# First query product of a fused attention and feed-forward kernel: plain loads ahead of transposing loads, chunk 0 transposed on TensorE, first product kept in SBUF

## The chip, the core and the metric

The kernel runs on one core of a Trainium2 chip. The core has TensorE (PE in the profile, with its weight loads as PEld), VectorE (DVE), ScalarE (ACT), GpSimd (POOL) and SyncE (SP), each with an instruction queue of its own that is worked off in order. Transfers are issued from the queues of SP, ACT and POOL. The metric is device time in microseconds (us) of one execution. Before the change three executions took 722.78, 722.94 and 723.15 us; the median is 722.94 us.

## The reference

All tensors are bf16; S = 2048 rows, D = 1024, 32 heads of 32, Df = 3584.

```python
qkv = (x @ wqkv)                       # 2048x1024 @ 1024x3072, cut into q, k, v
# each position attends to itself and 7 positions 2, 4, .. 14 rows back
logits = einsum("bhsd,bhswd->bhsw", q, kg) * scale
a = einsum("bhsw,bhswd->bhsd", softmax(logits), vg) @ wo
b = (gelu(x @ w_gate) * (x @ w_up)) @ w_down
g = sigmoid((x * gate_w).sum(-1, keepdims=True))
out = g * a + (1 - g) * b
```

## The kernel before

**Tiling.** The rows are cut into four chunks of 512. A contraction tile is 128 wide, so D has eight of them (kt 0 to 7). Matmuls take the transposed activations: `xs[c]` holds chunk c of x as eight 128x512 tiles.

**Fast products.** Every large product is done by a seven-product block scheme instead of eight: two blocks of rows (chunk 0 and chunk 1 for the first pair), two halves of the contraction, two halves of the columns. It needs sums and differences of blocks. For the activations these are T1 (`tf[:, 0]`, chunk 1 first half minus chunk 0 first half, L516), T2 (L518), T3 (L520) and T4 (L521), all on DVE (`x_forms`). For the weights they are four forms, each written by DVE in two instructions for the qkv weights (`qkv_forms`, L709). Partial results are carried from one product to another by copies: a PSUM bank is seeded with an earlier product, or a copy in SBUF is added on the way out.

**The first query product.** `first_pair` (L568) runs the scheme for q of chunks 0 and 1, over four column tiles t. In order: A, first half of the contraction (kt 0 to 3, L592); a copy of A into a second bank Bk, the seed (L602 on DVE, L604 on ACT); A, second half (kt 4 to 7); the gate's products of chunks 0 and 1 (`gate`, L874, with a transposing read of the bank by DVE, L880); then the products with T1 (Dk, copied to SBUF by L637), T2 (Bk, copied by L648), T3, the fourth weight form, and T4 (all matmuls at L772). After that follow k and v for the same chunks, the feed-forward pass of the first two chunks from about 84 us on, and the second pair.

**What feeds it.** Two plain loads (`load_rows`, L312, on SP's and ACT's queues) bring the first half of chunk 0's columns as rows; `turn_rows` (L543) transposes them on TensorE with an identity (L550), 16 transposes into four banks, one row tile each, and copies them out (L559, L561). `loads` (L424) then issues on SP's queue, in this order: the query weights kt 0-1 and kt 2-3 (512 KB each, L428), a transposing load of the second half of chunk 0 (L357), kt 4-5 and kt 6-7, two transposing loads of chunk 1 (L357), eight key weight tiles (L352), the value weights (L434) and the first rows of w_down (L387).

**The order of the work.** The instruction order on every engine is made when the kernel is built. `Weave.run` (L134) keeps eleven streams of operations, with an estimated cost and the dependencies of each, and emits the operation that could start earliest, with a bias per stream or operation and due times for the weight forms (`DUE`, L224). Each engine keeps that order. A change at the start therefore shifts the planner's clocks and can alter the order on DVE, ACT, SP and POOL in the rest of the kernel. In the second pair (from about 309 us) the stages repeat for chunks 3 and 2, with the sums L837 and L847 read out of the banks by DVE, and attention work (L937, L943, L1084, L1094) between them on the same queue.

Of the kernel before, what the change touches and what calls it, by code (L numbers as in the profile page):

```python
# [14 lines left out]
P = 128  # L15
# [139 lines left out]
def kernel(  # L155
# [152 lines left out]
    def xb_give(i, op):  # L308
        xb_free.append((i, op))

    def load_rows(q, j, hf):
        q.dma_start(out=hrow[:, XR + j:XR + j + 2, hf * KH * P:(hf + 1) * KH * P],  # L312
                    in_=x[j * P:(j + 2) * P, hf * KH * P:(hf + 1) * KH * P].rearrange("(j p) n -> p j n", p=P))

    load_rows(nc.sync, 0, 0)
    load_rows(nc.scalar, 2, 0)
    grow = xbuf[0:KT, 1, 0:P]
    nc.scalar.dma_start(out=grow, in_=gate_w.rearrange("(k p) -> k p", p=P))
    warm = xbuf[:, 0, 0:2]
# [32 lines left out]
            yield ring_load(("wqkv", c, which, kt), lambda g, kt=kt: nc.sync.dma_start(  # L352
                out=g.rearrange("p (k n) -> p k n", k=1), in_=qkv_src(which, kt, 1)), deps)

    def early_x(c):
        for hf in range(2) if c else (1,):
            o = Op("SP", (KH * P * SC * 2, 2.1), lambda hf=hf: nc.sync.dma_start_transpose(  # L357
                out=xq(c, hf), in_=x[c * SC:(c + 1) * SC, hf * KH * P:(hf + 1) * KH * P]), tail=1.2)
            yield o
            for k in range(KH):  # L360
                w.done[("x", 1, KH * hf + k) if c else ("pt", k, 1)] = o

    def load_x(c, deps):
        deps = deps + ([[("qk", 1)], [("att", 0)]][c - 2] if c > 1 else [])
# [8 lines left out]
    def load_prep(i0):  # L373
        n = min(2, NPREP - i0)
        kind, src, nr = ("d", B_w_down, FH) if i0 < FH else ("o", A_wo, NTH)
        r0 = i0 if kind == "d" else i0 - FH
        si = i0 // 2 % NSTG

        def fn():
            st = stage(si)  # L380
            for h, r in ((0, r0), (1, nr + r0)):
                if kind == "d":
                    v = src[r * P:(r + n) * P, :].rearrange("(k p) (h n) -> p k h n", p=P, h=2)
                else:
                    v = AP(src.tensor, src.offset + r * D, [[NT * D, P], [D, n], [NW, 2], [1, NW]])
                for k in range(n):
                    nc.sync.dma_start(out=st[:, 2 * h + k], in_=v[:, k])  # L387
        return Op("SP", (4 * n * P * NW * 2, 2.0 * n), fn, [("preps", i0 - 2 * NSTG)] if i0 >= 2 * NSTG else [("qkv", 1, 0, t) for t in range(NT)] if si == 2 else [("gcol",)] if si == 1 else [],
                  key=("prep", i0))

    def load_block(sup, b, first=()):
# [30 lines left out]
                    ([("stored", "o" if o else "d")] if name[0] == "T" else []) + [("w", 0, NBLK - 1, 3)] + list(first))  # L422

    def loads():  # L424
        for kt in range(0, KT, 2):
            if kt == KH:
                yield from early_x(0)
            o = Op("SP", (2 * P * D * 2, 0.7), lambda kt=kt: nc.sync.dma_start(  # L428
                out=qbuf[:, kt:kt + 2], in_=qkv_src(0, kt, 2)), key=("wqkv", 0, 0, kt))
            yield o  # L430
            w.done["wqkv", 0, 0, kt + 1] = o
        yield from early_x(1)
        yield from load_qkv(0, 1)
        yield Op("SP", (KT * P * D * 2, 1.0), lambda: [nc.sync.dma_start(out=vbuf[:, hf * KH:(hf + 1) * KH],  # L434
                                                                        in_=qkv_src(2, hf * KH, KH)) for hf in range(2)],
                 key=("wqkv", 0, 2))
        yield load_prep(0)
        yield load_prep(2)
        yield from load_block(0, 0)
        yield load_prep(4)  # L440
        yield from load_block(0, 1)
        for b in range(2, NBLK):
            yield from load_block(0, b)
            if 4 + 2 * (b - 1) < NPREP:
                yield load_prep(4 + 2 * (b - 1))
        for sup in range(NSUP):
            c0 = 2 * sup
            more = sup + 1 < NSUP
            if more:
                yield from load_down(c0)  # L450
                for n in range(3):
                    yield from load_qkv(c0 + 2, QVK[n], range(KT) if n == 0 else [k for i in range(KH) for k in (i, i + KH)],
                                        [("wq", c0 + 2, QVK[n - 1], 3, KH - 1)] if n else [])
                for b in range(NE // FB):
                    yield from load_block(sup + 1, b, [("wq", c0 + 2, QVK[2], 3, KH - 1)])
                yield from load_down(c0 + 1)
                for b in range(NE // FB, NBLK):
                    yield from load_block(sup + 1, b)
            else:
                yield from load_down(c0)  # L460
                yield from load_down(c0 + 1)
# [47 lines left out]
    def x_forms():  # L509
        t = tt(KH * SC)  # L510
        for sup in range(NSUP):
# [1 line left out]
            dx = [("x", max(ca, cb), kt) for kt in range(KT)]  # L513
            b12, b22, b11, b21 = xq(cb, 0), xq(cb, 1), xq(ca, 0), xq(ca, 1)
            free = [("ffn", sup - 1)] if sup else []
            t1 = dve(t, lambda b12=b12, b11=b11: V(out=tf[:, 0], in0=b12, in1=b11, op=ALU.subtract), dx[0:KH] + free, lag=0.5, key=("xf", sup, 1), bias=-1.0)  # L516
            yield t1
            t2 = dve(t, lambda b22=b22: V(out=tf[:, 1], in0=b22, in1=tf[:, 0], op=ALU.subtract), [t1] + dx[KH:], lag=0.5, key=("xf", sup, 2), bias=-1.0)  # L518
            yield t2
            yield dve(t, lambda b12=b12, b22=b22: V(out=b12, in0=b22, in1=b12, op=ALU.subtract), [("z", cb)], key=("xf", sup, 3), bias=-1.0 if sup else -0.3)  # L520
# [19 lines left out]
        yield halo_of(c, kT, 1)  # L540
        yield halo_of(c, vT, 2)

    def turn_rows():  # L543
        for j in range(NST):
            i, free = bank_take()
            pt = banks[i][:].bitcast(BF16)[:, 0:KH * P].rearrange("p (k s) -> p k s", k=KH)

            def go(pt=pt, j=j):
                for kk in range(KH):
                    nc.tensor.transpose(out=pt[:, kk, :], in_=xrow(j, kk, 1), identity=ident)  # L550
            o = Op("PE", 0.24, go, [free] if free else [], tail=0.17)
            yield o
            if j == NST - 1:
                gt = banks[i][:].bitcast(BF16)[:, KH * P:KH * P + KT]
                og = Op("PE", 0.1, lambda: nc.tensor.transpose(out=gt, in_=grow, identity=ident[0:KT, 0:KT]), [], tail=0.17)
                yield og
            dst = xs[0][:, 0:KH, j * P:(j + 1) * P]
            if j % 2:
                e = act(0.58, lambda pt=pt, dst=dst: nc.scalar.copy(out=dst, in_=pt), [o], key=("pt", j, 0))  # L559
            else:  # L560
                e = dve(0.42, lambda pt=pt, dst=dst: nc.vector.tensor_copy(out=dst, in_=pt), [o], key=("pt", j, 0))  # L561
            yield e
            if j == NST - 1:
                e = act(0.2, lambda: nc.scalar.copy(out=gcol[:], in_=gt), [og], key=("gcol",))
                yield e
            bank_give(i, e, True)

    def first_pair(c, prod, dst, ev, B11, B21, T1, T2, T3, B22, T4):  # L568
# [15 lines left out]
            return ap if t < 2 else two(ap)  # L584

        def mm(t, kts):
            d = [("wqkv", c, 0, kt) for kt in kts] + [("x", ca, kt) for kt in kts if ca]                 + [("pt", j, kts[0] // KH) for j in range(NST) if not ca]

            def go():
                for kt in kts:  # L590
# [7 lines left out]
        def seed(t):  # L598
# [6 lines left out]
            yield e  # L605
            ev["seed", t] = fr[t] = e

        if not c:
            for t in ts:
                A[t], fr[t] = bank_take(dirty=True)  # L610
            for kt in range(2):
                for t in ts:
                    yield mm(t, [kt])
        for t in ts:
            if c:
                A[t], fr[t] = bank_take()
            yield mm(t, range(KH) if c else [2, 3])
            yield from seed(t)
        if not c:
            for t in ts:  # L620
                yield mm(t, [KH, KH + 1])
        for t in ts:
            yield mm(t, range(KH, KT) if c else [KT - 2, KT - 1])
            out_, key, d = dst(1, 0, t)
            e = act(0.48, lambda t=t, out_=out_: nc.scalar.copy(out=out_, in_=banks[A[t]][:]), [at[t]] + d, key=key)
            yield e
            bank_give(A[t], e)
        for t in ts:
            if not c and t < 2:
                yield from gate(t)  # L630
            Dk[t], free = bank_take(dirty=t > 1)
            o = prod(Dk[t], 0, 0, T1, t, True, [free])
            yield o

            def cp(t=t):
                m5[t] = hold(t, 0, "m5")
                nc.scalar.copy(out=m5[t], in_=as_(t, banks[Dk[t]][:]))  # L637
            ev["m5", t] = act(0.48, cp, [o])
            yield ev["m5", t]
        for k in range(2):  # L640
            ring_give(("wqf", c, 0, 0, k), o)
        for t in ts:
            o = prod(Bk[t], 0, 1, T2, t, False, [ev["seed", t]])
            yield o

            def cp2(t=t):
                u2[t] = hold(t, 1, "u2")
                nc.scalar.copy(out=u2[t], in_=as_(t, banks[Bk[t]][:]))  # L648
            ev["u2", t] = act(0.48, cp2, [o])
            yield ev["u2", t]  # L650
        for k in range(2):
            ring_give(("wqf", c, 0, 1, k), o)
        for t in ts:
# [96 lines left out]
    def qkv_pair(c, whichs=QVK):  # L750
# [8 lines left out]
                return tmp(which, t), ("tmp", which, t), d  # L759
            return qkv_dst(ca if first else cb, which, t), ("qkv", ca if first else cb, which, t), d  # L760

        def prod(bk, which, form, rhs, t, start, deps):
            def fn():
                for kt in range(KH):
                    if isinstance(form, tuple):
                        hi, up = form
                        wv = qkv_w(c, which, kt + KH * hi)
# [8 lines left out]
            elif isinstance(form, tuple):  # L776
                d = raw_keys(c, which, range(KH * form[0], KH * form[0] + KH))
            else:
                d = [("wq", c, which, form, kt) for kt in range(KH)]
            sup = c // 2  # L780
            have = [[("x", ca, kt) for kt in range(KH * hf, KH * hf + KH)] if ca else [("pt", j, hf) for j in range(NST)] for hf in range(2)]
            d += {(0, 0): have[0], (1, 0): have[1],
                  0: [("xf", sup, 1)], 1: [("xf", sup, 2)], (0, 1): [("xf", sup, 3)], 3: [], (1, 1): [("xf", sup)]}[form]
            return pe(KH, fn, d + [x_ for x_ in deps if x_ is not None])

        if whichs == [0]:
            yield from first_pair(c, prod, dst, ev, B11, B21, T1, T2, T3, B22, T4)
# [609 lines left out]
            w.done[("down", c)] = o  # L1397

    def main():
        yield from turn_rows()  # L1400
        yield from qkv_pair(0, [0])
        yield from qkv_pair(0, [1])
        yield from gate_sum(0)
# [53 lines left out]
```

## Time and profile before

| what | value |
| --- | --- |
| median of three executions | 722.94 us |
| span of the profiled execution, first to last instruction | 720.1 us |
| PE busy | 710.1 us, 99% of the span |
| DVE busy | 609.8 us, 85% |
| ACT busy | 323.8 us, 45% |
| TensorE clock granted | full in all 40 slices |
| PE busy in the first 20.76 us | 15.85 us |
| DMA rate in 20.76 to 35.44 us | 374 GB/s |

The profiled execution's own time is its 720.1 us span and what lies around it; against the median 2.8 us lie outside. The page cuts the span into 40 slices of 18 us and gives each engine's busy tenths; the chain of work that ended last is followed back from the last instruction to what released each step. A busy PE in the first slice includes eight warm-up matmuls (3.43 us) on a zeroed tile.

### The profile page before, as it was taken

The page shows a single profiled execution, that of the slowest core. Times are in us where ns is not written, and L with a number is a line of the kernel's source. Part 1 is how long each engine was busy: PE and PEld are TensorE (multiplying, and loading weights), DVE is VectorE, ACT ScalarE, POOL GpSimd, SP SyncE. Part 2 cuts the span into 40 slices and gives each one's busy share as a digit, 9 for nine tenths or more (in the row PEclk, how much of TensorE's full clock was granted, in tenths as well). Part 3 has the DMA queues.
Part 4 walks back from the last instruction along what each step waited for, and adds up shares of the span by engine and source line. Part 5 has one row for each costly group of instructions (what it writes and reads, how often), then busy time and mean ns, then how long its engine had stood idle before and what let it go on. Part 6 is the DMA issues. An engine that isn't in the chain of part 4 may idle for free.

```text
span 720.1 us, 9892 instructions
## 1 busy us (share of the span) xinstructions
PE 710.1 (99%) x3337; PEld 342.7 (48%) x3337; DVE 609.8 (85%) x862; ACT 323.8 (45%) x547; POOL 73.8 (10%) x130
## 2 busy tenths in 40 slices
PE   7999999999999999999999999999999999999997
PEld 3556544444444444456554444444444444444443
DVE  4989999999998999799789988799999997849300
ACT  3354585555585522153465323258556655310110
POOL 0020333343121100100000000100000000001000
PEclk9999999999999999999999999999999999999999
DMA  9953899996797799943378899996647656999992
GB/s 263 363 192 97 248 295 311 362 317 225 179 249 230 238 253 330 336 174 117 88 214 272 277 299 352 311 310 186 185 137 194 172 165 161 322 294 376 297 338 93
DMA packets 184179, 176.84 MB, mean 246 GB/s; under 512 B 58304, under 2 KB 140224, under 8 KB 184000
## 3 DMA queue, kind: packets, MB, share of 16 engines
q1 hardware_dynamic: 174512, 145.53, 68.6%
q0 software_dynamic: 9328, 30.42, 11.6%
q8 instruction: 26, 0.43, 0.2%
q10 hardware_dynamic: 288, 0.26, 0.1%
q14 instruction: 25, 0.20, 0.1%
HBM read 132.12 MB, written 31.46 MB: 227 GB/s over the span
## 4 chain that ended last, share of the span: by engine, by line
PE 96%; DVE 1%; SPq 1%; DMA 1%; issue 0%; ACT 0%; DVEq 0%
PE ps L1136 47%; PE ps L1305 30%; PE ps L772 18%; PE ps L592 1%; SPq L357 1%; DMA hT<-in_A_wqkv_dram 1%; DVE ring L709 0%; SPq L428 0%; DVE lend L837 0%; DVE tf L518 0%; DVE zt L880 0%; PE ps L874 0%; ACT ost L1346 0%; DVE hT L709 0%; PE ps L898 0%
## 5 line engine op out<-in xcount | busy, mean ns | idle before, releaser
L1136 PEld LDWEIGHTS <-ring 128*128 128x128 bf16 x1568 | 153.2, 98 | 185.1 <-issue 0.5
L1136 PE MATMUL ps<-lend,ring 128*128 128x512 bf16 x896 | 212.7, 379 | 0.0
L1136 PE MATMUL ps<-tf,ring 128*128 128x512 bf16 x672 | 164.3, 379 | 0.0
L1305 PE MATMUL ps<-ring,hT 128*128 128x512 bf16 x708 | 160.7, 379 | 0.0
L1305 PEld LDWEIGHTS <-hT 128*128 128x128 bf16 x708 | 69.1, 98 | 83.8 <-DVE ost L1380 0.4
L1084 DVE TENSOR_TENSOR xbuf<-xbuf,lend 128x2048 bf16<-128x2048 bf16 x64 | 77.5, 1217 | 16.6 <-DMA xbuf<-xbuf 16.5
L772 PEld LDWEIGHTS <-ring 128*128 128x128 bf16 x512 | 65.0, 127 | 49.6 <-issue 3.6
L937 DVE TENSOR_TENSOR xbuf<-qo,lend 128x2048 bf16<-128x2048 bf16 x64 | 77.0, 1218 | 2.3 <-ACT lend L830 2.3
L943 DVE TENSOR_TENSOR xbuf<-xbuf 128x2048 bf16<-128x2048 bf16 x56 | 68.2, 1218 | 0.2
L772 PE MATMUL ps<-tf,ring 128*128 128x512 bf16 x256 | 58.4, 380 | 3.2 <-DVE lend L837 1.4
L772 PE MATMUL ps<-lend,ring 128*128 128x512 bf16 x256 | 57.9, 379 | 0.0
L1346 ACT ACTIVATE ost<-ps,omg 128x512 bf16<-128x512 f32 x16 | 11.0, 687 | 101.3 <-PE ps L1305 89.7
L1168 ACT COPY ps<-ps 128x512 f32<-128x512 f32 x56 | 32.1, 573 | 51.8 <-PE ps L1136 51.6
L1212 ACT ACTIVATE gl<-ps 128x512 bf16<-128x512 f32 x56 | 33.5, 598 | 46.5 <-PE ps L1136 46.3
L1305 PE MATMUL ps<-ring,qo 128*128 128x512 bf16 x192 | 49.3, 380 | 0.0
L1338 POOL DMA_DIRECT2D out_dram<-ost x24 | 13.0, 541 | 336.6 <-ACT ost L1346 248.3
L1185 DVE TENSOR_TENSOR hT<-hT,gl 128x1024 bf16<-128x1024 bf16 x56 | 38.3, 685 | 8.6 <-ACT hT L1178 8.5
L505 POOL DMA_DIRECT2D fforms<-ring x56 | 30.8, 551 | 144.2 <-DVE ring L496 138.1
L1224 DVE TENSOR_TENSOR u<-ps,u 128x512 f32<-128x512 f32 x56 | 38.3, 685 | 2.7 <-PE ps L1136 2.3
L1228 ACT ACTIVATE gl<-u 128x512 bf16<-128x512 f32 x56 | 35.4, 633 | 11.3 <-DVE u L1224 10.7
L1220 ACT COPY u<-ps 128x512 f32<-128x512 f32 x56 | 32.8, 586 | 14.3 <-PE ps L1136 14.3
L1094 DVE TENSOR_TENSOR xbuf<-xbuf 128x2048 bf16<-128x2048 bf16 x32 | 38.9, 1217 | 0.1
(120 smaller groups left out, 668.8 us busy)
## 6 DMA issues: line engine op xcount, KB each, us to landing
ring<-dforms SPq DMA_DIRECT2D x112, 256.0 KB, 5.0
ring<-in_B_w_down_dram SPq DMA_DIRECT2D x84, 256.0 KB, 5.4
ring<-in_B_w_gate_dram SPq DMA_DIRECT2D x56, 256.0 KB, 5.4
fforms<-ring POOLq DMA_DIRECT2D x56, 256.0 KB, 5.2
ring<-fforms SPq DMA_DIRECT2D x56, 256.0 KB, 4.1
ring<-in_B_w_up_dram SPq DMA_DIRECT2D x42, 256.0 KB, 4.8
ring<-in_A_wqkv_dram SPq DMA_DIRECT2D x32, 256.0 KB, 4.5
ring<-oforms SPq DMA_DIRECT2D x32, 256.0 KB, 5.6
```

What stands on the lines that cost most here:

```text
L772: nc.tensor.matmul(banks[bk][:], lhsT=lhsT, rhs=rhs[:, kt, :], start=(start and kt == 0), stop=(kt == KH - 1), skip_group_check=True)
L937: V(out=w3(box[t]), in0=q_b, in1=k_w, op=ALU.mult)
L943: V(out=w3(box[0]), in0=w3(box[0]), in1=w3(box[t]), op=ALU.add)
L1084: return dve(tt(n), taking(("p", t), lambda: V(out=w3(box["p", t]), in0=w3(box["ab"]), in1=v_w, op=ALU.mult)), [("qkv", c, 2, t), abo] + ( ...
L1094: V(out=p0.rearrange("p (u n) -> p u n", u=2), in0=lo, in1=hi, op=ALU.add)
L1136: nc.tensor.matmul(banks[bk][:], lhsT=wv[:, k, fl * P:(fl + 1) * P], rhs=rhs[:, k, :], start=(start and k == 0), stop=(k == KH - 1), skip_ ...
L1185: yield dve(tt(2 * SC), lambda hv=hv, gv=gv: nc.vector.tensor_tensor(out=hv, in0=hv, in1=gv, op=ALU.mult), [e, ev[f, "g1"], ev[f, "g2"]], ...
L1212: nc.scalar.activation(out=gl[f][:, r1 * SC:(r1 + 1) * SC], in_=banks[A[f]][:], func=ACT.Gelu_apprx_tanh)
L1220: nc.scalar.copy(out=u2[f][:], in_=banks[Bk[f]][:])
L1224: e = dve(tt(SC, True), lambda f=f: nc.vector.tensor_tensor(out=u2[f][:], in0=banks[Dk[f]][:], in1=u2[f][:], op=ALU.add), [o, ev[f, "u2"]])
L1228: ev[f, "g2"] = act(0.54, lambda f=f: nc.scalar.activation(out=gl[f][:, r2 * SC:(r2 + 1) * SC], in_=u2[f][:], func=ACT.Gelu_apprx_tanh), [ ...
L1305: nc.tensor.matmul(banks[bk][:], lhsT=l, rhs=wv[:, i, :], start=(start and k == 0), stop=(q == last and i == 1), skip_group_check=True)
```

## The change

- `loads` issues the query weights as eight loads of 256 KB, tile by tile. Between kt 3 and kt 4 a plain load brings the second half of chunk 0 as rows (512 KB, four row tiles), in place of the transposing load. The two transposing loads of chunk 1 stay behind all of these.
- `turn_rows(hf)` now turns one half at a time, and goes by contraction tile: four transposes fill one bank with tile kt of all 512 rows. The first half is copied out by DVE and ACT in turn, the second half, turned within `first_pair`, by DVE alone.
- A, first half, is copied to SBUF by ACT (`keep`, into the last rows of `hT`), not to a second bank. Four further ACT copies bring it from there into the banks Bk once the A banks are free. The two DVE seeds go.
- T1 of the first pair is made in two halves, and the T1 products of t = 0, 1 start on the first half. The gate's product of chunk 1 comes after them, and the T2 product of t = 0 comes ahead of the T1 product of t = 3.
- The first w_down rows wait for the seeds, the second ones for the last turned tile (the buffers are shared).

```diff
-    def early_x(c):
-        for hf in range(2) if c else (1,):
+    def early_x():
+        for hf in range(2):
...
     def loads():
-        for kt in range(0, KT, 2):
+        for kt in range(KT):
             if kt == KH:
-                yield from early_x(0)
-            o = Op("SP", (2 * P * D * 2, 0.7), lambda kt=kt: nc.sync.dma_start(
-                out=qbuf[:, kt:kt + 2], in_=qkv_src(0, kt, 2)), key=("wqkv", 0, 0, kt))
-            yield o
-            w.done["wqkv", 0, 0, kt + 1] = o
-        yield from early_x(1)
+                yield Op("SP", (KH * P * SC * 2, 0.6), lambda: load_rows(nc.sync, 0, NST, 1), key=("xr", 1))
+            yield Op("SP", (P * D * 2, 0.5), lambda kt=kt: nc.sync.dma_start(
+                out=qbuf[:, kt:kt + 1], in_=qkv_src(0, kt, 1)), key=("wqkv", 0, 0, kt))
+        yield from early_x()
...
-            t1 = dve(t, lambda b12=b12, b11=b11: V(out=tf[:, 0], in0=b12, in1=b11, op=ALU.subtract), dx[0:KH] + free, lag=0.5, key=("xf", sup, 1), bias=-1.0)
-            yield t1
+            for k0, n_, key in ((0, KH, ("xf", sup, 1)),) if sup else ((0, KH // 2, ("xfa", sup)), (KH // 2, KH // 2, ("xf", sup, 1))):
+                t1 = dve(tt(n_ * SC), lambda b12=b12, b11=b11, k0=k0, n_=n_: V(
+                    out=tf[:, 0, k0:k0 + n_], in0=b12[:, k0:k0 + n_], in1=b11[:, k0:k0 + n_], op=ALU.subtract),
...
-    def turn_rows():
-        for j in range(NST):
+    def turn_rows(hf):
+        for kk in range(KH):
             i, free = bank_take()
...
+            def go(pt=pt, kk=kk):
+                for j in range(NST):
+                    nc.tensor.transpose(out=pt[:, j * P:(j + 1) * P], in_=xrow(j, KH * hf + kk, 1), identity=ident)
+            o = Op("PE", 0.24, go, ([free] if free else []) + ([("xr", 1)] if hf else []), tail=0.17)
...
             yield mm(t, range(KH) if c else [2, 3])
-            yield from seed(t)
+            if c:
+                yield from seed(t)
+            else:
+                def keep(t=t):
+                    late[t] = hrow[:, FT - 4 + t, :].bitcast(F32)
+                    nc.scalar.copy(out=late[t], in_=banks[A[t]][:])
+                fr[t] = ev["kept", t] = act(0.48, keep, [at[t]])
+                yield fr[t]
         if not c:
-            for t in ts:
-                yield mm(t, [KH, KH + 1])
+            yield from turn_rows(1)
+            for kt in (KH, KH + 1):
+                for t in ts:
+                    yield mm(t, [kt])
...
+            for t in ts:
+                Bk[t], free = bank_take(True)
+                ev["seed", t] = act(0.5, lambda t=t: nc.scalar.copy(out=banks[Bk[t]][:], in_=late[t]), [ev["kept", t]] + ([free] if free else []))
+                yield ev["seed", t]
+            w.done["seeded",] = ev["seed", KH - 1]
+            for kts in ((0, 1), (2, 3)):
+                for t in ts[:2]:
+                    yield from first5(t, kts)
+            yield from gate(1)
+            yield from first5(2)
+            yield from second6(0)
+            yield from first5(3)
+            for t in ts[1:]:
+                yield from second6(t)
```

## The prediction

> **What bounds the kernel now.** I read the slices first. PE is busy in every slice but the first and the last, at full clock.
>
> ```profile
> PE   7999999999999999999999999999999999999997
> DVE  4989999999998999799789988799999997849300
> PEclk9999999999999999999999999999999999999999
> ```
>
> So time can be won where PE waits. PE's own waits after 20 us are two small ones in the second pair, behind DVE's sums, and the one that ends at 20.76 us:
>
> ```profile
> PE ps L772 <- DVE lend L837: 1.4, 2, 0.9
> PE ps L772 <- DVE zt L880: 0.8, 1, 0.8
> ```
>
> The chain of waits of the first 60 us (start, length, what) shows what sets 20.76 us: SP's queue and transfers to 12.73, then DVE without a gap, then PE alone.
>
> ```profile
> 2.27 4.97 SPq L357
> ...
> 7.28 0.58 SPq L428
> ...
> 7.90 4.83 DMA hT<-in_A_wqkv_dram
> ...
> 12.83 1.90 DVE ring L709 x3
> 14.72 0.60 DVE hT L709
> ...
> 17.01 1.18 DVE tf L518
> ...
> 18.72 1.28 DVE ring L709 x2
> ...
> 20.09 0.64 DVE zt L880
> ...
> 20.76 39.01 PE ps L772 x180
> ```
>
> The timeline of PE shows its work ahead of that, with the idle time and what ended it in brackets:
>
> ```profile
> 6.16 3.61 PE L592 MATMUL ps<-lend,hT 128*128 128x512 bf16 x16 [0.67 <-ACT lend L559]
> 11.28 3.67 PE L592 MATMUL ps<-lend,hT 128*128 128x512 bf16 x16 [1.50 <-DMA hT<-in_A_wqkv_dram]
> 16.52 1.05 PE L772 MATMUL ps<-tf,ring 128*128 128x512 bf16 x4 [1.02 <-DVE tf L516]
> 18.05 1.92 PE L772 MATMUL ps<-tf,ring 128*128 128x512 bf16 x8
> ```
>
> From 20.76 PE does the last 68 of the q matmuls and ends the q pair at 35.44: 0.216 us each. What ends q earlier ends the kernel earlier, as long as the later order adds no wait.
>
> **The transfers.** Adding each issue's start to its time to landing: query weights kt 0-1 land at 1.25 + 4.7 = 5.95, kt 2-3 at 1.76 + 5.6 = 7.36, the transposing load of chunk 0 at 2.27 + 7.0 = 9.27, kt 4-5 at 7.28 + 4.0 = 11.28, kt 6-7 at 12.73, chunk 1's halves at 8.41 + 6.4 = 14.8 and 12.6 + 4.2 = 16.8. So 512 KB plain behind another cost 1.41 and 1.45, and 512 KB transposed 1.91, 2.07 and 2.0. kt 4-5 took 2.01 behind the transposing load, 0.58 too long: SP had been held 4.97 us in that load's issue and issued them only at 7.28.
>
> The change puts a plain 512 KB in place of the transposed one (2.0 - 1.43 = 0.57 saved), and nothing on SP holds the weights back (0.58 saved). kt 7 then lands at 12.73 - 1.15 = 11.6, chunk 1 at 13.6 and 15.6. The plain rows land at 7.36 + 1.43 = 8.8. SP issues nine loads where two weight loads and a transposing one stood; at 0.49 us each (eight key loads in 3.90) it is through at 5.8, ahead of the data, so the count costs nothing; if the queue were no longer ahead, each would cost its 0.49. The key weights behind the transposing loads start when the second issue ends, about 1.1 us earlier than 14.81.
>
> [...]
>
> **PE and DVE up to q's end.** All times below are in the profile's clock.
> First half: the rows of ACT's queue land at 0.74 + 3.8 = 4.54, 16 transposes take 1.07 (L550), so A starts at about 5.7; eight matmuls to 7.4, kt 3 landed at 7.36, eight more to 9.2 (3.61 for 16).
> Added: 16 transposes, 1.07, to 10.3. They lie in the time in which PE stood 1.50 for kt 4-5 before; without that cover they would cost their 1.07.
> DVE copies the four turned tiles one after the other (0.42 each, L561) from 9.65 on, to 11.3; the first query weight form follows (0.61), the second starts at 11.9. It stood at 12.83. The data (11.6) is no longer its limit, the copies are. Gain 0.93. If copies follow each other faster than their 0.42, as L709 does (0.61 apart at 0.69 long), it is 1.1; if the rows, which come in shorter pieces, cost 2.0 like a transposed load, kt 7 lands at 12.2 and the gain is 0.5.
> From there DVE's order is as before, in which 7.93 us lie from that form to PE's restart at 20.76. Splitting T1 (1.22 for one) costs a second start, about 0.07. Chunk 1's first half (13.6) is there when DVE comes to T1 at 14.4, its second half (15.6) when it comes to T2 at 16.1. The second gate read then frees its bank at 11.9 + 7.93 + 0.07 = 19.9.
> PE meanwhile: A's second half 10.3 to 14.0 (3.67), gate 0.61; T1's first half is ready at 15.05; T1 products of t = 0, 1 by 16.85 (four times two matmuls, 1.73), second gate to 17.5, t = 2 to 18.3, then the T2 product of t = 0 (0.86) to 19.2, which before came after the wait. T2 is made by 17.3. PE waits 0.7 for the bank and restarts at 19.9 with 64 matmuls left, not 68: 64 x 0.216 = 13.8, end at 33.7. Against 35.44 the gain is 0.86 + 0.86 = 1.7 us.
>
> ACT gains work: four keeps and four seeds of 0.57 in place of two copies, with the four q copies between them. The last q copy ends at about 14.7, the first seed at 15.3, the last at 17.0; they are wanted at 18.3 and after 20.8, and the first Dk copy queued behind them is ready only at 17. Cover 3.0 us on the first seed; beyond it each us costs one. DVE loses two copies of 0.70. The w_down rows that now wait for the seeds (17.0) were issued at 20.73, behind the value weights; 1.1 us off that is still later than 17.0, so nothing.
>
> **Later.** PE's order is the same after the first pair. On DVE, ACT, SP and POOL the order is replanned. k's forms had their last key weights at about 23.9 (issued 18.2, 5.7 to landing) and k starts at 35.44; DVE idles 2.29 us at 40.0 to 42.3, so k and v keep up with a PE that comes 1.7 earlier. In the second pair the operations in the changed order between the first q form (before at 308.65) and the first L837 add up to 35.2 us by the rows of before, against 35.1: the wait of 0.94 there stays. It could go, with the 0.44 at 369 (-1.4); or DVE could come later by one attention transposing issue (two took 5.03), +2.5. I take 0, because the sums agree. POOL's stores have nobody waiting at once.
>
> Sum: 720.1 - 1.7 = 718.4 span; the 2.8 us around it stay, so 722.9 - 1.7 = 721.2.
>
> **Rivals.**
> 1. The start gains little. For: chunk 1's transposing loads now stand behind 3.1 MB of plain data, and T1 has 0.8 us of slack on them. If they land at their old 14.8 and 16.8, T1 starts 0.4 later than I have it, T2 0.7 later; with the rows at 2.0 us as well, 0.5 to 0.9 of the gain is left: 722.2. Against: the landings are evenly spaced behind one another in one queue.
> 2. More than I count: both waits behind L837 go too. 721.2 - 1.4 = 719.8. For: the query weights of the second pair are now loaded ahead of two attention transposing loads, before behind them. Against: T2 of the second pair comes behind later pieces of chunk 3 now, so DVE starts no earlier.
> 3. Slower: a new wait in the second pair. The last two value weight tiles stand on SP behind two transposing loads that wait for the probabilities on DVE. I place these at 316, the two issues take 5.03, landing about 5 later, 326; DVE's form wants them at about 328.6. Slack 2.5; every further us moves L837, and PE already waits there, so it costs one. It decides above 2.5 + 1.7 = 4.2 us late; 6 late gives 721.2 + 3.5 = 724.7. Against: no such slip of SP in the profile of before, whose loads end their waits at DVE forms, not at PE.
>
> **How the numbers follow.** The main case has 0.55, its own range 720.4 to 722.0 (start gain from 0.9 to 2.5). Rival 1 has 0.21, rival 2 0.13, rival 3 0.11. A measurement tells about 0.2%, 1.45 us, from no change, so faster means under 721.5: 0.41 of the main case and rival 2, together 0.54; slower than 724.4 is most of rival 3, 0.10; the rest, 0.36, is within. The range reaches over rival 2 to 719.5 and over rival 1 to 723.1, the slowest of the three executions before (a start that gains nothing); it leaves out rival 3 and the far ends of the others.
>
> **What would show it.** In the changed profile: kt 7 landing near 11.6 and chunk 1 at 13.6 and 15.6; no PE gap but one of about 1 us behind T1 and one of 0.7 behind the gate's read; the continuous PE work starting near 19.9; the q pair ending near 33.7; L837's waits at 1.4 in all. I am wrong if chunk 1 lands after 14.5, if DVE's copies end after 11.9, if a seed stops PE, or if PE waits more than 3 us between 300 and 385.

## The result and the profile after

The changed kernel takes 731.98 us (median of four executions, 730.47 to 732.63) against 723.02 us (722.78 to 723.15) for the kernel before: the ratio is 1.012, with a 95% interval of 1.0108 to 1.0132. It is slower by 9 us, where 721.2 was forecast. The profiled execution took 732.51 us with a span of 730.7 us, 10.6 more than the 720.1 us of before.

Lines of the changed kernel stand some 40 further down: L772 is now L812 (matmuls of q, k and v), L592 is L595 (the first product), L709 is L749 (DVE's weight forms), L657 and L667 are L697 and L707 (DVE's sums of the q products), L837 is L877, L880 is L920, L1075 is L1115 and L1136 is L1176.

The slices of the page after, PE and the clock granted to it:

```profile
PE   9889999999999999999999999989999999999998
...
PEclk9989999999999999999999999999999999999999
```

Slices 2, 3 and 27 (about 18 to 55 and 475 to 493 us) stand a tenth lower on PE than before, and slice 3 has lost a tenth of its clock. PE's waits after (total, times, longest, all in us) name the places:

```profile
PE ps L812 <- DVE qo L697: 4.9, 1, 4.9
PE ps L1176 <- ACT m L1234: 2.5, 1, 2.5
PE ps L595 <- ACT ps L607: 1.3, 1, 1.3
...
PE ps L812 <- DVE zt L920: 0.6, 1, 0.6
```

The two waits behind L837 (now L877) are gone. Three new ones have come, and the largest lies inside the q pair, which the prediction had down as free of waits after its restart. DVE's timeline there (start, length, instruction, in brackets the idle time before it and what ended it):

```profile
27.35 0.68 DVE L697 TENSOR_TENSOR qo<-ps,hT 128x512 bf16<-128x512 f32 x1
37.21 0.69 DVE L749 TENSOR_TENSOR ring<-ring 128x1024 bf16<-128x1024 bf16 x1 [9.18 <-DMA ring<-in_B_w_gate_dram]
37.82 0.68 DVE L697 TENSOR_TENSOR qo<-ps,hT 128x512 bf16<-128x512 f32 x1
```

DVE makes three of the four T3 sums (the last of the three is the first line), then reaches a *key* weight form, and that form waits 9.18 us for a load of *w_gate*, which it neither reads nor writes. The fourth sum is queued behind it, and PE's last T4 product waits for that sum:

```profile
30.88 2.75 PE L812 MATMUL ps<-tf,hT 128*128 128x512 bf16 x12
38.56 1.87 PE L812 MATMUL ps<-tf,hT 128*128 128x512 bf16 x4 [4.92 <-DVE qo L697]
```

The table of windows shows a second loss behind the first. Its columns are the window, its length, busy time and count of PE, PEld, DVE, ACT and POOL, then the granted clock, DMA share and GB/s:

```profile
33.50:38.50 5.00, 0.14 (x1) 0.00 (x0) 1.29 (x3) 0.58 (x1) 0.00 (x0) 0.92 0.77 201
38.50:44.00 5.50, 5.44 (x13) 2.12 (x13) 5.46 (x11) 1.28 (x3) 0.00 (x0) 0.50 0.35 118
44.00:46.00 2.00, 2.00 (x9) 0.94 (x8) 1.93 (x4) 1.03 (x2) 0.93 (x2) 0.88 0.25 92
46.00:52.00 6.00, 6.00 (x29) 3.66 (x28) 5.28 (x8) 2.93 (x5) 4.98 (x7) 1.00 0.84 279
```

After the gap PE is always busy, but at a granted clock of 0.50: 13 matmuls in 5.5 us, where the same window of before has 27. The small matmuls that close k (L898 before, L938 after) start at 66.60 us in place of 59.70. That window and the close of k in the kernel before, then the close of k after:

```profile
38.50:44.00 5.50, 5.50 (x27) 3.40 (x26) 3.15 (x5) 3.30 (x6) 3.38 (x5) 1.00 1.02 368
```

```profile
59.70 0.31 PE L898 MATMUL ps<-zq,qsum 128*32 128x4 f32 x16
```

```profile
66.60 0.31 PE L938 MATMUL ps<-zq,qsum 128*32 128x4 f32 x16
```

The 6.9 us between the two are made of -1.1 from a shorter start (without the gap the q pair would end at 30.88 + 16 x 0.216 = 34.3, before it ended at 35.44), +4.9 of waiting, and about +3 of low clock (from 38.56, less 0.86 for the last four q matmuls, PE takes 27.2 us to 66.60; before, from 35.44, it took 24.3).

The other 3.7 us are lost later. PE gains the 0.94 and 0.44 of the waits that went, and loses 1.33 near 321 us, 2.46 near 478 us, and the low clock behind that (16 matmuls in 5.14 us where 16 x 0.216 is 3.46: 1.7): 4.1 net, by the profile's lines.

So there were two questions. Why does a key form wait for w_gate, and is this what costs the time? And where do the later waits come from?

### The profile page after: what moved, and what is told of

Same layout as the page of the kernel before. It is cut to its first block, busy times and chain, and to the rows that moved or that the text cites. A ratio compares the mean times of both kernels' runs of the same rounds, so it can differ in the third digit from the quotient of the medians.

```text
span 730.7 us, 9958 instructions
## 1 busy us (share of the span) xinstructions
PE 716.7 (98%) x3353; PEld 345.0 (47%) x3353; DVE 610.6 (84%) x865; ACT 326.0 (45%) x553; POOL 73.8 (10%) x130
## 4 chain that ended last, share of the span: by engine, by line
PE 89%; DMA 5%; SPq 2%; DVE 2%; issue 1%; ACT 1%; DVEq 0%
PE ps L1176 45%; PE ps L1345 28%; PE ps L812 16%; DMA hT<-in_B_w_down_dram 1%; SPq L357 1%; DMA xbuf<-xbuf 1%; DMA ring<-in_B_w_gate_dram 1%; DMA ring<-dforms 1%; DMA ring<-in_A_wqkv_dram 1%; DVE xbuf L1124 1%; DMA hT<-in_A_x_dram 1%; DVE ring L749 0%; SPq L1115 0%; SPq L352 0%; SPq L428 0%
## 5 line engine op out<-in xcount | busy, mean ns | idle before, releaser
L1176 PEld LDWEIGHTS <-ring 128*128 128x128 bf16 x1568 | 153.8, 98 | 188.7 <-issue 5.3
L1176 PE MATMUL ps<-lend,ring 128*128 128x512 bf16 x896 | 213.2, 380 | 2.5 <-ACT m L1234 2.5
L1176 PE MATMUL ps<-tf,ring 128*128 128x512 bf16 x672 | 165.5, 381 | 0.0
L812 PEld LDWEIGHTS <-ring 128*128 128x128 bf16 x512 | 65.2, 127 | 49.3 <-issue 5.0
L812 PE MATMUL ps<-tf,ring 128*128 128x512 bf16 x256 | 59.0, 381 | 1.0 <-DVE zt L920 0.6
L812 PE MATMUL ps<-lend,ring 128*128 128x512 bf16 x256 | 59.6, 387 | 0.0
L1268 ACT ACTIVATE gl<-u 128x512 bf16<-128x512 f32 x56 | 35.5, 633 | 10.6 <-DVE u L1264 10.3
L1260 ACT COPY u<-ps 128x512 f32<-128x512 f32 x56 | 32.8, 586 | 14.5 <-PE ps L1176 14.5
```

The lines of the kernel that those rows point to most:

```text
L812: nc.tensor.matmul(banks[bk][:], lhsT=lhsT, rhs=rhs[:, kt, :], start=(start and kt == 0), stop=(kt == KH - 1), skip_group_check=True)
L1176: nc.tensor.matmul(banks[bk][:], lhsT=wv[:, k, fl * P:(fl + 1) * P], rhs=rhs[:, k, :], start=(start and k == 0), stop=(k == KH - 1), skip_ ...
L1260: nc.scalar.copy(out=u2[f][:], in_=banks[Bk[f]][:])
L1268: ev[f, "g2"] = act(0.54, lambda f=f: nc.scalar.activation(out=gl[f][:, r2 * SC:(r2 + 1) * SC], in_=u2[f][:], func=ACT.Gelu_apprx_tanh), [ ...
```

## The experiments

**The theory of the slot.** The program's instructions show that the form that waits (the third of the four key forms, the one written in place, for contraction tiles 2 and 3) reads its two tiles through one access pattern. `raw` (in `qkv_forms`) builds it with a stride that is the distance between the slots in which the tiles happen to lie: `[[w1.offset - w0.offset, 2], ...]`. Ring slots are handed out in the order in which the planner emits the loads and forms. In the changed order tiles 2 and 3 lie in slots 2 and 4. Slot 3, between them, first held a query form, was given back, and then went to the w_gate load A11. The wait is there as if the pattern touched everything from its first byte to its last, slot 3 too. In the kernel before, the two tiles lie in slots 3 and 5, and slot 4 holds another key form that DVE itself writes, so the form has no DMA to wait for. Rival: the wait named is incidental, and the replanned order of DVE, SP and ACT is what costs. The first four kernels are compared with 722.96 us of the kernel before (13 executions).

**a_slots: two slots change places in the changed kernel.** The order of instructions on all queues stays that of the changed kernel; the slot handed out fourth is 4 and the fifth is 3, so tiles 2 and 3 are neighbours.

```diff
-    ring_free = [(i, ()) for i in range(NG)]
+    ring_free = [(i, ()) for i in [0, 1, 2, 4, 3] + list(range(5, NG))]
```

> The changed kernel with two slots of the weight ring swapped, so that key weight tiles 2 and 3 lie next to each other; nothing else differs on any queue. Theory W: DVE's third key form waits for the first w_gate load only because its access runs over the ring slot between the two tiles, which that load fills. Then DVE's wait of 9.2 us, PE's of 4.9 and the low clock after it go: the pair of k ends about 7 us earlier, the time falls from 732.0 to about 724.5, and PE's wait of 2.5 us near 480 stays. Rival L: the w_gate load is needed, or the transfers are late as such; then PE waits at least 3 us in another place before 66 us and the time stays above 729.

Measured: 724.82 (721.96 to 727.18, nine executions), ratio to before 1.0023 (1.0005 to 1.0041). The waits of its PE:

```profile
PE ps L1176 <- ACT m L1234: 2.3, 1, 2.3
PE ps L595 <- ACT ps L607: 1.8, 1, 1.8
...
PE ps L812 <- DVE zt L920: 0.9, 1, 0.9
PE ps L812 <- DVE tf L515: 0.6, 1, 0.6
```

The 4.9 is gone with nothing but two slot numbers changed: 7.2 of the 9 us. The two later waits have stayed, so they do not come from the first.

**b_slots: the same wait planted in the kernel before.**

```diff
-    ring_free = [(i, ()) for i in range(NG)]
+    ring_free = [(i, ()) for i in [4, 1, 2, 3, 0] + list(range(5, NG))]
```

Again the order of all queues is untouched. The pattern of a key form now spans the slot of A12, the w_gate load behind A11.

> The kernel before with two ring slots swapped, so that the slot between its key tiles 2 and 3 is the one that a w_gate load takes; every queue's order is that of before. Theory W: DVE's second key form kt 2 now waits for that load, which lands near 38.7; all four sums of the q pair stand behind it, PE waits about 7 us from 32 on and then runs at a low clock for some 3 us more: about 733. Rival L: slots do not matter, 723.0.

Measured: 733.8 (733.39 to 733.84), ratio 1.0147 (1.0132 to 1.0162). One wait on PE answers for it, and behind it one of DVE for the w_gate load:

```profile
PE ps L772 <- DVE qo L657: 9.1, 1, 9.1
```

```profile
38.62 1.90 DVE L709 TENSOR_TENSOR ring<-ring 128x1024 bf16<-128x1024 bf16 x3 [13.05 <-DMA ring<-in_B_w_gate_dram]
```

It is the second key form that waits here, and all four sums stand behind it. Nothing of the change is in this kernel, and it is 10.8 us slower. The small matmul that closes k comes at 70.44 in place of 59.70, 10.74 later: what is lost at 32 us is still lost at the end. That the slot between the two tiles makes the wait, and the wait the loss, is so shown from both sides.

**a_zeros: PE is kept at work through the gap.** The changed kernel, with twenty matmuls of zero weights behind the third T4 product, which is in the middle of the 4.9 us.

```diff
+            if not c and t == 2:
+                def still(bk=Bk[2]):
+                    for _ in range(20):
+                        nc.tensor.matmul(banks[bk][:], lhsT=warm[:, 0:1].to_broadcast([P, P]), rhs=T4[:, 0, :], start=False, ...)
```

> The changed kernel with 20 matmuls of zero weights added to the T4 product of t = 2, that is ahead of PE's wait of 4.9 us; they add nothing to the result. Theory C: after an idle gap that long PE is granted half the clock for some us, which cost 2.9 us in k; with the gap cut to about 0.6 us the clock stays full and the time falls by about 2.9 to 729.1, though PE does 4.3 us of work more. Rival D: k's matmuls are slow because operands come late after the wait; then the time stays 732.0.

The timeline of PE and a window:

```profile
33.30 4.48 PE L717 MATMUL ps<-tf,xbuf 128*128 128x512 bf16 x20
38.97 1.02 PE L822 MATMUL ps<-tf,hT 128*128 128x512 bf16 x4 [1.20 <-DVE qo L697]
...
64.97 0.31 PE L948 MATMUL ps<-zq,qsum 128*32 128x4 f32 x16
```

```profile
38.50:44.00 5.50, 4.52 (x21) 2.65 (x21) 5.50 (x10) 2.31 (x4) 0.00 (x0) 1.00 0.31 96
```

The clock stays at 1.00, and the stretch from the end of the wait to k's last matmul takes 26.00 us (with a wait of 0.51 in it) in place of 28.04. The total is not as clear: 731.34, ratio 1.0117 (1.0078 to 1.0155). Two executions with a mean granted clock of 0.999 or more took 728.47 and 729.88 us, two below that 732.8 and 734.95; the last is the profiled one, with later waits of 3.2 and 3.1 us where the changed kernel has 2.5 and 1.3. The median lies between the two expectations. So the clock's part is shown in the stretch, 2.0 to 2.6 us, and open in the total.

**a_order: the order of before is written in.** a_slots, and from the first T3 product of the q pair on the planner's choices are replaced by the list of choices that it made in the kernel before; the slots of the second pair's first form are given back where they were. The whole changed start remains.

```diff
+            if left[0] <= SYNC:
+                si = rest[0][0]          # the stream that came next in the kernel before
+                s = [z for z in live if z[3] == si][0]
...
+            for k in range(2):
+                ring_give(("wqf", c, 0, 0, k), w.done["first5", c])
             for t in ts:
                 yield from second6(t)
```

> The swapped slots again, and from the T3 products of the first q pair on all queues keep the order of the kernel before, with the ring slots of the second pair given back where they were. Theory O: what is lost beyond the first wait, about 3.9 us near 480, comes from the replanned order; without it the start's gain of about 1.1 us is left: 721.6 to 722.1. Rival S: the later wait comes from the earlier start itself; then 724 or more, as with the slots alone.

Measured: 720.31 (719.1 to 720.83), ratio 0.9952 (0.9935 to 0.997): faster than both kernels, and below the theory's own range. (The ratio alone would be 3.5 us, the medians are 2.65 apart, the spans 1.5: the kernel before took from 721.91 to 726.41 us there.) Its waits and three lines of its PE timeline (its lines stand another 54 further down):

```profile
PE ps L866 <- DVE lend L931: 1.7, 1, 1.7
PE ps L374 <- DVE xbuf L372: 0.9, 1, 0.9
PE ps L866 <- DVE zt L974: 0.6, 1, 0.6
```

```profile
5.67 3.78 PE L647 MATMUL ps<-lend,hT 128*128 128x512 bf16 x16
...
19.89 3.61 PE L866 MATMUL ps<-tf,ring 128*128 128x512 bf16 x15 [0.60 <-DVE zt L974]
...
57.97 0.31 PE L992 MATMUL ps<-zq,qsum 128*32 128x4 f32 x16
```

k closes at 57.97 in place of 59.70: in this execution the start is worth 1.73 us. (The same start closes k at 58.33 in a_late and at 58.78 in a_slots, so 0.9 to 1.7.) And the rest of the loss, a_slots' 724.8 against 720.3, is the replanned order.

What in that order? The transposing transfers of the attention of the first two chunks are issued later in a_slots. First the SP timeline of before, then that of a_slots:

```profile
273.65 3.82 SPq L1006 DMA_TRANSPOSE xbuf<-xbuf  x1
296.09 5.03 SPq L1075 DMA_TRANSPOSE xbuf<-xbuf  x2
```

```profile
287.51 6.14 SPq L1046 DMA_TRANSPOSE xbuf<-xbuf  x1
315.84 3.38 SPq L1115 DMA_TRANSPOSE xbuf<-xbuf  x2
```

They come 14 and 20 us later, and the work of DVE that needs them with them. From 20 to 310 us a_slots' DVE has done 267.3 us of work by the table of windows, where it did 274.6 before and does 274.8 in a_order; 7.0 of the difference lie in the window from 260 to 310, first before, then a_slots:

```profile
260.00:310.00 50.00, 50.00 (x245) 22.69 (x243) 43.20 (x61) 10.95 (x17) 3.78 (x7) 1.00 1.05 316
```

```profile
260.00:310.00 50.00, 49.74 (x239) 22.98 (x243) 36.20 (x53) 9.38 (x17) 4.34 (x8) 1.00 1.04 310
```

DVE's queue comes there to an output row that waits for PE. Before, attention work fills the time up to it; in a_slots most of that work comes later. Again before, then a_slots:

```profile
288.56 0.75 DVE L1380 SCALAR_TENSOR_TENSOR ost<-ps,omg,m5d 128x512 bf16<-128x512 f32 x1 [0.65 <-PE ps L1305]
```

```profile
287.71 0.75 DVE L1420 SCALAR_TENSOR_TENSOR ost<-ps,omg,m5d 128x512 bf16<-128x512 f32 x1 [7.72 <-PE ps L1345]
```

So DVE reaches the second pair with a debt of 7 us. The next four kernels (compared with 723.08 us of before, 13 executions) ask what order and slots are worth apart, where the debt is made, and what terms of the start are worth.

**a_order_only: the order of before, but the slots of the changed kernel.** It is a_order without the line of a_slots.

```diff
-    ring_free = [(i, ()) for i in [0, 1, 2, 4, 3] + list(range(5, NG))]
+    ring_free = [(i, ()) for i in range(NG)]
```

> The changed kernel with the order of before written in on all queues, but with the ring slots handed out as in the changed kernel; DVE's in-place key form now spans the slot of the next w_gate load (A12, behind A11 on SP's queue). Theory 'slot' (the false wait on a load is a loss of its own that no order heals): PE idle 6 to 9 us between 33 and 43 ahead of a sum behind DVE, granted clock near 0.50 after it, and with the 720.3 of the kernel that has both order and slots, 720.3 + 8 to 11 = 728 to 731. Rival 'order alone' (the order of before is what heals, the slots matter only with the new order): within 1 us of 720.3.

Measured: 732.04 (730.89 to 732.21), ratio 1.0124 (1.0109 to 1.014), just above the theory's range. One wait, what DVE waits for, and the window behind it:

```profile
PE ps L866 <- DVE qo L751: 9.3, 1, 9.3
```

```profile
38.20 1.90 DVE L803 TENSOR_TENSOR ring<-ring 128x1024 bf16<-128x1024 bf16 x3 [12.87 <-DMA ring<-in_B_w_gate_dram]
```

```profile
43.00:44.00 1.00, 1.00 (x4) 0.34 (x3) 1.00 (x3) 0.24 (x1) 0.00 (x0) 0.50 0.24 68
```

The order alone heals nothing. Here the pattern spans the slot of A12. DVE goes on at 38.20 in place of 37.21, only 1 us later than in the changed kernel; PE's wait is twice as long because, as in b_slots, it is the second form that waits and not the third, with all four sums behind it and not one. So the slot costs 7.2 us with the new order and 11.7 with the old one, and the order costs 4.5 us with the mended slots and nothing measurable with the others (731.98 against 732.04). Either is a loss of its own, but their prices do not add up.

**a_late: the new order for 300 us, then the order of before.**

```diff
-SYNC = 1810
+SYNC = 1080
```

> Slots swapped, the new order of the changed kernel kept up to the first operations of the second pair (near 303 us), from there the order of before written in. Theory 'the later order costs' (SP's weight loads and transposes of the second pair in other places): the waits of 1.8 near 321 and 2.3 near 480 go, time as with the whole order of before, 720 to 721. Rival 'the first 300 us cost' (the work that the new order leaves behind at 300 us is what comes late afterwards): one of the two waits at least stays, 723 to 725.

Measured: 731.18 (730.26 to 731.9), ratio 1.0115 (1.01 to 1.013). Both ranges were too low; the sign is the rival's. Its waits lie between 310 and 339 us:

```profile
PE ps L866 <- DVE qo L751: 4.1, 1, 4.1
PE ps L866 <- DVE ring L803: 2.7, 1, 2.7
PE ps L647 <- ACT ost L1440: 2.2, 1, 2.2
```

The order of before is not better from 300 us on by itself; it fits the work that the order of before has left at 300 us. Where the attention is late, DVE still has it to do up to 319 us, and holding to before's sequence makes PE wait 9 us. That the new order's two waits near 321 and 478 are what is left of the same debt is argued from this, not run. The debt is made in the first 300 us. The plans themselves tell two things more, read from the emitted instructions and not run. With the order of before prescribed only up to about 54 us (by the planner's clock) the planner goes on nearly as in a_slots; prescribed up to about 186 us it returns to the order of before by itself. And giving the second pair's slots back at the old place, alone, changes the order of no queue.

**a_pairs: the query weights in four loads.** a_order, with pairs of tiles as before the change.

```diff
-        for kt in range(KT):
+        for kt in range(0, KT, 2):
...
-                out=qbuf[:, kt:kt + 1], in_=qkv_src(0, kt, 1)), key=("wqkv", 0, 0, kt))
+                out=qbuf[:, kt:kt + 2], in_=qkv_src(0, kt, 2)), key=("wqkv", 0, 0, kt))
```

> Order of before and swapped slots, and the query weights loaded in pairs of tiles as before (four loads instead of eight), so that no issue on SP has to wait for the load eight back. Theory 'semaphore' (the 0.9 to 1.1 us in which SP stands before the fifth weight load hold all later landings back): SP issues the transposing loads of chunk 1 near 5 instead of 6.4, chunk 1 lands up to 1 us earlier, DVE's copies become the limit; the wait for the second gate's read shrinks from 0.6 by up to 0.5: 719.8 to 720.3. Rival (the DMA engines are full anyhow, the wait on SP is hidden): the landings stay where they are, 720.3 within 0.3; a pair landing later than its first tile alone costs up to 0.7: 721.0.

Measured: 719.35 (718.65 to 720.11), ratio 0.9953 (0.9938 to 0.9967). SP's timeline shows the transposing loads issued at 4.52, where a_order has them at 6.42:

```profile
2.78 1.11 SPq L480 DMA_DIRECT2D hT<-in_A_wqkv_dram  x2
4.52 8.45 SPq L409 DMA_TRANSPOSE lend<-in_A_x_dram  x2
```

The first lands 9.3 us after its issue, at 13.8; in a_order it takes 7.6, to 14.0. So 1.9 us on the queue became 0.2 at the landing: the transfers move 372 GB/s from 4 to 8 us and 324 from 8 to 13, the queue's stand is hidden, and PE restarts at 19.79 against 19.89. Landings and restart are the rival's, though the median lies below both ranges. The ratios of the two kernels are equal, so neither is shown to be the better.

**a_t2last: the first T2 product goes back behind the last T1 product.** The rest is a_order.

```diff
             yield from first5(2)
-            yield from second6(0)
             yield from first5(3)
-            for t in ts[1:]:
+            for t in ts:
                 yield from second6(t)
```

> Order of before and swapped slots, but the first T2 product goes back behind the last T1 product on PE, as before the change. The prediction's term for this step is 0.86 us (four matmuls of 0.216 in the wait for the gate's read): PE idle ahead of the last T1 product is 1.4 to 1.5 in place of 0.6, and the time 0.9 above 720.3, 721.2. Rival (the products behind wait for DVE at the next place anyhow): the gap grows, but the wait of 1.7 behind DVE in the second pair shrinks by as much, 720.3 within 0.3.

Measured: 721.31 (719.84 to 723.69, ten executions), ratio 0.9974 (0.9958 to 0.999). The median is 1.0 above a_order, the two intervals overlap a little. The wait for the gate's second read:

```profile
PE ps L865 <- DVE zt L973: 1.5, 1, 1.5
```

It is 1.5 where a_order has 0.6, 0.9 for the four matmuls; the wait in the second pair is 1.0 in place of 1.7 in this execution.

**b_zeros: b_slots with PE at work through its 9.1 us.** 38 matmuls of zero weights stand behind the last B22 product. This asks for the price of the clock in a kernel whose executions scatter little.

```diff
+            if not c and t == 3:
+                def still(bk=Dk[3], fn=o.fn):
+                    fn()
+                    for _ in range(38):
+                        nc.tensor.matmul(banks[bk][:], lhsT=warm[:, 0:1].to_broadcast([P, P]), rhs=B22[:, 0, :], start=False, ...)
```

> The kernel before with the planted wait (key tiles in slots that span a load's slot: PE idle 9.14, 733.8 us), and 38 matmuls with weights of zero put behind the last B22 product of the q pair, so that PE works through 8.2 of the 9.1 us. They add nothing to the sum in their bank. Theory 'clock' (the idle gap itself costs its length, and the low clock after it costs more: 15 matmuls took 5.17 us behind the planted gap where 16 take 3.62): PE comes out of the wait at the same time, near 41.2, with a granted clock of 1.00, and the time falls by 1.5 to 2 us to 731.8 to 732.3. Rival (the granted clock is only a sign, work behind the gap waits for DVE anyhow): the clock stays at 1.00 and the time stays within 0.4 of 733.8.

Measured: 732.55 (731.65 to 733.41), ratio 1.0139 (1.0118 to 1.0159), beside its own 722.21 of before. From its PE timeline:

```profile
41.93 3.68 PE L779 MATMUL ps<-tf,hT 128*128 128x512 bf16 x16 [0.95 <-DVE qo L657]
...
46.72 1.02 PE L779 MATMUL ps<-lend,ring 128*128 128x512 bf16 x4 [0.24 <-DVE qo L674]
...
70.12 0.31 PE L905 MATMUL ps<-zq,qsum 128*32 128x4 f32 x16
```

From the end of the wait to k's close it takes 28.19 us, b_slots 29.28: 1.1 saved in the stretch, of the 1.5 to 2 expected, since a new wait of 0.24 for DVE comes in. The total is 1.25 lower by the medians, 0.6 by the ratios, and the intervals overlap. So the gap's length is most of what the planted wait costs. The low clock adds, by the stretches, something over 1 us behind the 9.1 us gap and 2.0 to 2.6 behind the 4.9 us gap of the changed kernel.

## Why the prediction was wrong

**The transfers.** SP was to be through its nine loads at 5.8. In the profile after, it stands 1.1 us before the fifth weight load for an earlier transfer:

```profile
SPq L428 <- DMA hT<-in_A_x_dram: 1.1, 1, 1.1
```

The transfers issued by SP and ACT take eight semaphores in turn in the program as built, and each issue waits for the transfer that had its semaphore last, here one of ACT's two first loads. The prediction did name the case in which the queue is not ahead, but not this cause. Chunk 1's first half lands at 6.73 + 7.9 = 14.6, not 13.6, and the second at 16.6, not 15.6, nearly as before (14.8 and 16.8); so in this execution the 1.15 us saved did not reach them. "I am wrong if chunk 1 lands after 14.5" came about, yet cost nothing here: DVE reaches T1 at 14.92 and T2 at 16.76 without waiting (in a_slots and a_order_only T2 waits 0.17), and a_pairs shows that the stand itself is hidden.

**PE and DVE up to the restart.** The links of this chain were right, its times only in the best case. In a_order the first product starts at 5.67 (predicted 5.7), T1 at 14.28 (14.4), PE restarts at 19.89 (19.9), and k closes 1.73 us earlier (1.7). The T2 term, 0.86, is 0.9 in a_t2last's gap. But a_order is the earliest of the six profiled executions with this start: the restarts lie from 19.89 to 20.88, half of them at or above 20.52. In the changed kernel itself all of this is later by 0.6 to 0.8 (6.44, 14.92 and 20.52), although its instructions up to there are the same: its first 16 transposes took 1.98 us, where a_order has 1.31 and the prediction 1.07. The close agreement of a_order is therefore in part luck. So is the 11.9 for the second weight form: DVE's copies follow 0.34 apart, not 0.42, and end at 11.1, while kt 7 lands at about 5.9 + 5.9 = 11.8, not 11.6, so in a_order it is the load and not the copies that sets the form's start.

**"k and v keep up with a PE that comes 1.7 earlier."** This is the step that failed, worth about 8 us of PE's time (4.9 of waiting, 3 of low clock); a_slots, without the wait, is 7.2 us faster. The prediction took the key weights' landing (23.9) and an idle time of DVE (2.29 at 40 to 42) as proof of slack. It priced instructions, loads and their order, but not the storage: a new order hands out ring slots in a new sequence, and with them new neighbours inside a strided pattern. The dependency on the w_gate load was visible in the changed program's instructions, as a wait on a DMA in a form that had none before; no view of the profile of before could show it. Nor was the granted clock of 0.50 behind the 4.92 us gap priced.

**The second pair, "I take 0, because the sums agree."** Here a second step failed. The sum compared DVE's work between two points and took for granted that DVE reaches the first of them with as little left over as before. The waits behind L837 did not stay, as the sum had it, but went, as in rival 2. But the attention transfers of the first two chunks came 14 and 20 us later in the new plan, DVE had 7 us of work more left over at 310 us (a_slots), and in the changed kernel PE waited at other places, 1.33 and 2.46 us with the low clock behind the latter. a_slots against a_order prices the replanned order at 4.5 us.

**The rivals.** Rival 3 had the sign, and its place on SP came true: in a_slots the two transposes are issued at 315.84 (forecast 316), with the last two value weight loads behind them at 320.21. But DVE is nowhere idle for those weights (its only wait for weights from 305 to 345 us is 0.29, at 307.5), and the largest loss lies at 33 us; that a_slots' 724.8 is near rival 3's 724.7 is chance. Rival 1 is right about the landings, which cost at most the 0.17 of T2. With the old order and the mended slots the changed start is worth, by the medians, more than was forecast: a_order's 720.3 and a_pairs' 719.4 stand at and 1 us under the lower end of the main case, 720.4. The traces show 0.9 to 1.7 us of that at k's close; where the rest comes from is open. (The 2.8 us that the sum puts around the span are 1.8 in every execution whose span is on record; the other 1.0 is the profiled execution before being a faster one than the median.)

## What to carry to other kernels

Where storage is handed out in the order of a plan, any change of that order changes who lies beside whom. Compare the waits of the new program's instructions with the old one's, above all waits on a DMA in an instruction that reads no fresh load, before pricing anything else; and keep tiles that one strided pattern reads in adjoining slots. A gap on PE cost more than its length here (2.0 to 2.6 us on top of the 4.92, up to k's close), and a planner that replans the rest of a kernel after a small change at its start can lose more than the change wins: hold the old order fixed and measure the change alone.

## What the runs showed of the hardware

Behind some gaps on PE the matmuls ran at a granted clock of 0.50, and in these runs the length of the gap tells only roughly behind which. Gaps of 4.07 (a_late), 4.92 (the changed kernel), 9.14 (b_slots) and 9.35 us (a_order_only) all brought 0.50. Behind 3.10 and 3.23 us (both a_zeros) the length of the matmuls shows the same: 4 of them took 1.86 us behind the first, where 4 took 1.87 at 0.50 in the changed kernel and take 1.02 at 1.00; behind the second, 16 took 5.14, where 16 x 0.216 is 3.46. Gaps of 2.30 (a_slots) and 2.46 us (the changed kernel) near 475 brought 0.50 too, here a_slots after its 2.30:

```profile
474.00:475.00 1.00, 1.00 (x4) 0.32 (x3) 1.00 (x2) 0.00 (x0) 0.00 (x0) 0.50 1.27 384
```

Gaps of 1.75 (a_order), 1.78 (a_slots) and 2.17 us (a_late) left it at 1.00, and so did one of 2.74 us in a_late, which ends at 320.19:

```profile
321.00:322.00 1.00, 1.00 (x5) 0.52 (x6) 0.91 (x2) 0.42 (x1) 0.00 (x0) 1.00 0.07 16
```

Nor does its duration go by the gap: by the mean clocks of the windows, 0.50 lasted 3.2 us after the restart behind the 9.14 us gap, 5.4 behind the 9.35 us gap and 5.9 behind the 4.92 us gap. What decides whether it comes and how long it lasts was not shown. With matmuls with zero weights in the gap the clock stayed at 1.00 in both kernels that had them (a_zeros in all windows from 30 to 62 us, b_zeros from 28 to 60).
